# A fused attention and mixture-of-experts kernel: the four parts of a chunk's scatters moved from consecutive attention units to every second one

## The chip, the cores and the metric

The kernel runs on one core of one Trainium2 chip, as one program without collectives. The metric is the device time of one launch in microseconds (us), median over runs. One run is also profiled, and every row below comes from that profiled execution.

## What is computed

Eight sequences of 2496 tokens go through an attention with squared-ReLU scores, whose result is multiplied by `u`. All 19968 rows that come out are then sorted to one of 8 experts each. Every expert is a two-layer network, and its output is scaled by two gates and put back at the token's row.

```python
scores = (1.0 / S) * np.matmul(z, z.transpose(0, 2, 1))      # S = 2496, z: 8 x 2496 x 64
attn = np.maximum(scores, 0.0) ** 2
x = (u * np.matmul(attn, v)).reshape(B * S, D)               # D = 256
logits = x @ w_gate                                          # 8 experts
e_idx = np.argmax(logits, axis=1)
gate_w = softmax(logits)[e_idx]
eom = 1.0 / (1.0 + np.exp(-(x @ w_output_gate)))
for e in range(8):
    mask = e_idx == e
    h = np.maximum(x[mask] @ w1[e], 0.0)                     # 1024 hidden columns
    out[mask] = gate_w[mask, None] * eom[mask, e, None] * (h @ w2[e])
```

## The kernel before

**Attention stage.** A batch is cut into 5 chunks of queries (448 queries in chunk 0, 512 in the others), and a chunk is worked through in 10 units, one for every 256 keys. That makes 8 x 5 x 10 = 400 units. In a unit TensorE computes scores (L270, L271), or takes mirrored ones that were stored earlier (`take`, L355 and L385), and multiplies earlier scores with `v` (`weigh`, L403). ScalarE (ACT) applies ReLU (L272) and the square (L275) and rounds to the high half (L277, L385). VectorE (DVE) computes the low half (L281, L389). Scores are made two units ahead of the unit that weighs them.

**The tail of a chunk.** When a chunk's 10 units are done, an object of class `Tail` takes its output through a list of small steps, while the units of the next chunk run. The loop over the units calls `advance` of every live tail once per unit, just after that unit's `weigh`. Steps 0 to 9 run in the next chunk: multiply with `u` (`gate`), split, turn the rows (`rows`, L470, into the tile `xr`, of which there are two buffers), gate logits, choice of the expert (`pick`, L490 on ACT among others), `factor` (L531 and L535 on ACT), `place` (a small matmul, L556) and `scatter`, which works out each token's row number (L574). Step 10 is empty.

**The scatters.** Steps 11 to 14 are the four parts, so they fall into units 1, 2, 3 and 4 of the chunk after that. A part casts a quarter of the row numbers to integers on ACT (L581, tile `idx`, 8 buffers) and then issues four indirect DMAs on GpSimd (POOL, L585; three in two of the parts of a chunk 0). Each writes 128 rows of `xr` to `xs`, the array in memory from which the experts later load their tokens.

**What sets the order.** Every engine gets its instructions in the order in which the Python code writes them. SP issues the ordinary DMAs. GpSimd issues nothing but these scatters during attention, apart from a few preparations at the start. A step list `later` spreads the last two tails over the beginning of the expert stage.

**Expert stage.** Slots of up to 512 tokens load rows of `xs` (`load_x`, L921 and L929), and run the two layers. The first two slots' rows are already loaded inside the last two chunks of attention (units 4 of chunks 3 and 4 of the last batch). A scatter that comes behind such a load in the program waits for the load to land, as both touch `xs`.

Of the kernel before, what the change touches and what calls it, by code (L numbers as in the profile page):

```python
# [59 lines left out]

REST = S - (NCH - 1) * CH - 2 * P

TAIL = 15

N_HELD = 2

# [10 lines left out]
def attention_moe(ctx, tc, zt, zq_in, ut, v, wg, w12, out):  # L77
# [336 lines left out]
    class Tail:  # L414
# [183 lines left out]
        def advance(self):  # L598
            k = self.step
            self.step += 1  # L600
            (
                self.gate,
                lambda: (self.split(0), self.split(1)),
                self.rows,
                self.logits,
                self.turn,
                self.choose,
                self.pick,
                self.factor,
                lambda: (self.finish(), self.place()),  # L610
                self.scatter,
                lambda: None,
                lambda: self.scatter_part(0),
                lambda: self.scatter_part(1),
                lambda: self.scatter_part(2),
                lambda: self.scatter_part(3),
                lambda: None,
            )[min(k, TAIL)]()


    def t1(name, shape, dt=F32, tag=None):
        return pool.tile([1] + shape, dt, name=name, tag=tag or name)
# [247 lines left out]
    def pads():  # L870

        pad = pool.tile([P, ROW], F32, name="pad", tag="lt")
        nc.gpsimd.memset(pad, 0.0)
        nc.gpsimd.memset(pad.bitcast(I32)[:, SEG - 1 : SEG], NOTOK)
        ends = t1("ends", [E], I32)
        nc.vector.tensor_copy(out=ends, in_=carry[0][0:1])
        yield
        for e in range(E + 1):
            if e < E:
                at = nc.sync.value_load(ends[0:1, e : e + 1], min_val=e * CAP, max_val=e * CAP + N)  # L880
                seg = xs_rows[bass.ds(at, TW), :]
            else:
                seg = xs_rows[E * CAP : E * CAP + TW, :]
            it = nc.sync.dma_start(
                out=seg.rearrange("(p q) d -> p q d", q=4), in_=pad.unsqueeze(1).to_broadcast([P, 4, ROW])
            )
            tc.add_to_no_dep_group(last_scatters, it.ins)
            yield
# [291 lines left out]
    def prepare(k):  # L1180
        while to_load and to_load[0][0] - to_load[0][1] <= k:
            to_load.pop(0)[2].load()
        while to_split and to_split[0][0] <= k:
            to_split.pop(0)[2].split()

    attn = {}
    tail = nxt = o = None
    tails = []
# [23 lines left out]
    for k, (b, c, jp) in enumerate(units):  # L1212
# [33 lines left out]
        if pos == NPAIR - 1:  # L1246
            tail = nxt
            tails = [it for it in tails if it.step < TAIL] + [tail]
        prepare(k)
# [1 line left out]

    idle = lambda: None
    later = [idle] * (4 * 12)
    for k in (0, 2, 6, 10, 14):
        later[k] = tails[0].advance
    for k in (*range(1, 22, 2), 22, 29, 32, 35):
        later[k] = tail.advance
    more, fill = other_tables(), pads()
    for _ in range(29):
        later += [idle, lambda: next(more, None)]  # L1260
# [73 lines left out]
    with tc.If(used > N_MAIN + 1):  # L1334
        part = slots[last + 1 :]
# [63 lines left out]
```

## Time and profile before

| What | Value |
|---|---|
| Median of 3 runs | 2200.44 us (2196.61 to 2205.82) |
| The profiled execution's own time | 2191.03 us |
| Its span, first to last instruction | 2189.2 us |
| Mean granted TensorE clock | 0.999 of full speed |
| TensorE matmuls busy | 2163.7 us, 99% of the span |
| DVE busy | 1752.4 us, 80% |
| ACT busy | 1452.0 us, 66% |
| GpSimd busy | 940.2 us, 43% |

Busy times say how long an engine had an instruction in work, and idle time of an engine counts only where a busier one waits for it. The views used below are the page's totals, busy times by stretch of time, the list of who waited for whom, the durations and waits of one line of the kernel, and the timeline, which shows instructions in order with the idle time before them in brackets and what ended it.

### The profile page before, as it was taken

The numbers are of one execution on the slowest core, as the hardware profiler recorded it, in microseconds if no ns is written. First come the engines' busy times: TensorE is split into PE (matmuls) and PEld (weight loads), VectorE is DVE, ScalarE is ACT, GpSimd is POOL, SyncE is SP. The second block draws the span as 40 slices with busy tenths as digits, with TensorE's granted clock in tenths as the row PEclk, the third lists the DMA queues.
The fourth block names the chain that finished last, engine by engine and source line by source line (L and its number), as shares of the span: only waits on it lengthen the run. The fifth ranks groups of instructions, "written<-read, shape, count | busy, mean of one in ns | idle before, by whom it ended". The sixth has DMA issues, their size and how long they took to land. (4 is left out here: it accounts for less than half of the span.)

```text
span 2189.2 us, 35155 instructions
## 1 busy us (share of the span) xinstructions
PE 2163.7 (99%) x10207; PEld 1828.4 (84%) x10207; DVE 1752.4 (80%) x2884; ACT 1452.0 (66%) x2494; POOL 940.2 (43%) x829
## 2 busy tenths in 40 slices
PE   9999999999999999999999999999999999999998
PEld 7888788788788788888788888888888898888998
DVE  8898898898898898898898897676666766666676
ACT  8768768768778767767768765555555555555565
POOL 1365565565565564665565574321212111121222
PEclk9999999999999999999999999999999999999999
DMA  6695795794785785784784694535566766666542
GB/s 211 210 240 169 215 242 167 215 241 167 222 235 171 222 232 166 223 234 166 217 239 163 216 266 114 150 95 154 178 188 188 217 210 200 198 187 201 184 148 79
DMA packets 467738, 423.88 MB, mean 194 GB/s; under 512 B 156077, under 2 KB 366638, under 8 KB 467536
## 3 DMA queue, kind: packets, MB, share of 16 engines
q1 hardware_dynamic: 439952, 379.97, 59.3%
q0 software_dynamic: 27584, 41.58, 5.5%
q8 instruction: 82, 1.34, 0.3%
q14 instruction: 120, 0.98, 0.1%
HBM read 292.21 MB, written 158.66 MB: 206 GB/s over the span
## 5 line engine op out<-in xcount | busy, mean ns | idle before, releaser
L585 POOL DMA_INDIRECT xs<-xr,idx x624 | 766.1, 1228 | 597.8 <-ACT idx L581 422.1
L403 PE MATMUL o<-ah,v 128*128 128x512 f32 (+1 forms) x3200 | 845.8, 387 | 9.0 <-ACT ah L277 6.9
L403 PEld LDWEIGHTS o<-ah,v 128*128 128x128 f32 x3200 | 596.1, 188 | 120.7 <-ACT ah L277 10.7
L403 PE MATMUL o<-al,v 128*128 128x512 f32 (+1 forms) x1520 | 463.8, 386 | 0.5
L1012 ACT ACTIVATE hh<-sc 128x512 fp32r<-128x512 f32 (+7 forms) x328 | 190.1, 580 | 391.1 <-PE sc L1003 348.8
L1125 POOL DMA_INDIRECT out<-y,meta x156 | 159.0, 1019 | 629.1 <-ACT y L1115 558.3
L1013 DVE SCALAR_TENSOR_TENSOR hl<-sc,hh 128x512 fp32r<-128x512 f32 (+7 forms) x328 | 218.2, 665 | 262.3 <-ACT hh L1012 248.5
L1003 PE MATMUL sc<-xh,w 128*128 128x512 f32 (+8 forms) x1440 | 399.0, 362 | 1.8 <-issue 1.8
L1058 PE MATMUL o<-hh,w 128*128 128x512 f32 (+7 forms) x1184 | 400.2, 379 | 0.0
L403 PEld LDWEIGHTS o<-al,v 128*128 128x128 f32 x1520 | 283.9, 188 | 58.6 <-DVE al L281 6.6
L281 DVE TENSOR_TENSOR al<-a,ah 128x1024 fp32r<-128x1024 f32 (+1 forms) x199 | 233.1, 1171 | 111.0 <-ACT ah L277 91.0
L1003 PEld LDWEIGHTS sc<-xh,w 128*128 128x128 f32 x1440 | 258.2, 188 | 40.6 <-issue 1.3
L272 ACT ACTIVATE a<-sc 128x512 f32<-128x512 f32 (+1 forms) x398 | 207.6, 572 | 105.9 <-PE sc L271 44.1
L1058 PEld LDWEIGHTS o<-hh,w 128*128 128x128 f32 x1184 | 221.2, 188 | 38.9
L957 DVE TENSOR_TENSOR w<-raw,w 128x512 fp32r<-128x512 f32 x368 | 246.1, 680 | 2.8 <-ACT w L956 2.2
L1058 PE MATMUL o<-hl,w 128*128 128x512 f32 (+7 forms) x592 | 224.5, 379 | 0.0
L956 ACT CAST w<-raw 128x512 fp32r<-128x512 f32 x368 | 220.1, 615 | 0.0
L385 ACT CAST ah<-z 128x1024 fp32r<-128x1024 f32 x192 | 199.5, 1047 | 20.9 <-DMA z<-td 17.3
L275 ACT ACTIVATE a<-a 128x1024 f32<-128x1024 f32 (+1 forms) x199 | 203.6, 1023 | 6.3
L1003 PE MATMUL sc<-xl,w 128*128 128x512 f32 (+8 forms) x720 | 202.3, 362 | 0.0
L389 DVE TENSOR_TENSOR al<-z,ah 128x1024 fp32r<-128x1024 f32 x160 | 194.5, 1216 | 8.3 <-ACT ah L385 3.8
L270 PE MATMUL sc<-z,hl 128*128 128x512 f32 (+1 forms) x398 | 152.8, 384 | 5.0 <-ACT a L272 4.2
(201 smaller groups left out, 2395.5 us busy)
## 6 DMA issues: line engine op xcount, KB each, us to landing
raw<-in_w SPq DMA_DIRECT2D x368, 256.0 KB
z<-td SPq DMA_DIRECT2D x647, 128.0 KB
td<-t SPq DMA_DIRECT2D x160, 512.0 KB
raw<-in_v SPq DMA_DIRECT2D x80, 256.0 KB
u<-in_ut SPq DMA_DIRECT2D x32, 512.0 KB
ym<-yd SPq DMA_DIRECT2D x126, 128.0 KB
sx<-xs SPq DMA_DIRECT2D x120, 128.0 KB
yd<-yt SPq DMA_DIRECT2D x30, 512.0 KB
```

The costliest lines, as they stand in the source:

```text
L272: nc.scalar.activation(out=a[:, q, :w], in_=sc[:, :w], func=AF.Relu)
L275: nc.scalar.activation(out=a[:, :, :w], in_=a[:, :, :w], func=AF.Square)
L281: nc.vector.tensor_tensor(out=al[:, :, :w], in0=a[:, :, :w], in1=ah[:, :, :w].bitcast(F32), op=ALU.subtract)
L385: nc.scalar.copy(out=ah, in_=z)
L389: nc.vector.tensor_tensor(out=al, in0=z, in1=ah.bitcast(F32), op=ALU.subtract)
L403: nc.tensor.matmul(out=o[d][:, :w], lhsT=vv[:, q, d * P : (d + 1) * P], rhs=rhs, start=begins and q == 0 and k == 0, stop=ends and q == 1 ...
L585: it = nc.gpsimd.indirect_dma_start(out=xs[:, :], out_offset=bass.IndirectOffsetOnAxis(ap=idx[:, n - first : n - first + 1], axis=0), in_= ...
L956: nc.scalar.copy(out=ww[:, 0], in_=wr)
L957: nc.vector.tensor_tensor(out=ww[:, 1], in0=wr, in1=ww[:, 0].bitcast(F32), op=ALU.subtract)
L1003: nc.tensor.matmul(out=hp[:, at : at + n], lhsT=wb[2 * d + f // 4][:, ww, fs], rhs=xx[:, d, :], start=k == 0, stop=k == 5,)
L1013: nc.vector.scalar_tensor_tensor(out=lo, in0=hp[:, 0:used], scalar=0.0, in1=ho.bitcast(F32), op0=ALU.max, op1=ALU.subtract)
L1058: nc.tensor.matmul(out=y, lhsT=st, rhs=mv, start=f == 0 and k == 0, stop=f == 7 and k == 2)
```

## The change

The list of steps in `advance` gets three more empty steps, one before each of the parts 1, 2 and 3. In the attention stage the parts then stand at steps 11, 13, 15 and 17, that is at units 1, 3, 5 and 7 of the chunk. The last two tails, which run in the expert stage, get their parts by direct calls at the same places of `later` at which they stood before.

```diff
-TAIL = 15
+TAIL = 18
...
                 self.scatter,
                 lambda: None,
                 lambda: self.scatter_part(0),
+                lambda: None,
                 lambda: self.scatter_part(1),
+                lambda: None,
                 lambda: self.scatter_part(2),
+                lambda: None,
                 lambda: self.scatter_part(3),
                 lambda: None,
             )[min(k, TAIL)]()
...
     later = [idle] * (4 * 12)
-    for k in (0, 2, 6, 10, 14):
-        later[k] = tails[0].advance
-    for k in (*range(1, 22, 2), 22, 29, 32, 35):
+    for k in range(1, 22, 2):
         later[k] = tail.advance
+    for part in range(4):
+        later[2 + 4 * part] = lambda part=part: tails[0].scatter_part(part)
+        later[(22, 29, 32, 35)[part]] = lambda part=part: tail.scatter_part(part)
```

On ACT the casts `idx<-row` of the parts 1, 2 and 3 come later. This is chunk 0 of batch 4, from unit 4 to unit 7. `a`, `z` and `ah` are scores, `dl` and `hot` belong to the tail of the chunk before. Before:

```order
L581 ACTIVATE idx<-row 128x4
L272 ACTIVATE a<-sc 128x448 x2
L275 ACTIVATE a<-a 128x2x448
L197 CAST z<-raw 128x512
L367 ACTIVATE z<-sc 128x192 x2
L369 ACTIVATE z<-z 128x2x192
L387 CAST ah<-z 128x2x448
L490 ACTIVATE ex<-dl 128x128
L272 ACTIVATE a<-sc 128x448 x2
L275 ACTIVATE a<-a 128x2x448
L277 CAST ah<-a 128x2x448
L531 COPY both<-hot_103 64x136
```

And the same stretch after the change:

```order
L275 ACTIVATE a<-a 128x2x448
L581 ACTIVATE idx<-row 128x4
L197 CAST z<-raw 128x512
L367 ACTIVATE z<-sc 128x192 x2
L369 ACTIVATE z<-z 128x2x192
L387 CAST ah<-z 128x2x448
L490 ACTIVATE ex<-dl 128x128
L272 ACTIVATE a<-sc 128x448 x2
L275 ACTIVATE a<-a 128x2x448
L277 CAST ah<-a 128x2x448
L581 ACTIVATE idx<-row 128x4
L531 COPY both<-hot_103 64x136
```

The cast that closed unit 4 (part 3) now stands in unit 7, directly ahead of the copy L531, and part 2 stands in unit 5. The order on TensorE, VectorE, SP and GpSimd is the same in both kernels.

On GpSimd one thing differs all the same, in the last batch, where a scatter comes behind the first load of an expert's rows. The piece shows the scatters of chunk 3 of that batch with the semaphores that each waits for (`DMAHW`: loads that SP issued, `DMASW`: earlier scatters, `Activation`: the cast):

```order
 L585 DMA xs<-xr,idx 657408x66 [waits DMASW6_49]
 L585 DMA xs<-xr,idx 657408x66 [waits DMASW7_49]
-L585 DMA xs<-xr,idx 657408x66 [waits DMASW0_49,Activation_49]
-L585 DMA xs<-xr,idx 657408x66 [waits DMASW1_49]
-L585 DMA xs<-xr,idx 657408x66 [waits DMASW2_49]
-L585 DMA xs<-xr,idx 657408x66 [waits DMASW3_49]
-L585 DMA xs<-xr,idx 657408x66 [waits DMASW4_49,Activation_49]
-L585 DMA xs<-xr,idx 657408x66 [waits DMASW5_49]
-L585 DMA xs<-xr,idx 657408x66 [waits DMASW6_49]
-L585 DMA xs<-xr,idx 657408x66 [waits DMASW7_49]
 L585 DMA xs<-xr,idx 657408x66 [waits DMAHW2_49,DMAHW1_49,DMAHW6_49,DMAHW0_49,DMAHW7_49,DMASW0_49,Activation_49]
```

The wait for the load moves from the first scatter of the next chunk's tail eight rows up, to the first scatter of part 2 of this one, since parts 2 and 3 now come behind the load.

## Rows read from the trace of the kernel before

**Rows 1.** The page's first part: busy time, share of the span, instructions.

```profile
PE 2163.7 (99%) x10207; PEld 1828.4 (84%) x10207; DVE 1752.4 (80%) x2884; ACT 1452.0 (66%) x2494; POOL 940.2 (43%) x829
```

**Rows 2.** Busy times, attention stage: us, PE, PEld, DVE, ACT, POOL, clock, DMA.

```profile
30.00:1318.00 1288.00, 1275.49 (x5787) 1064.05 (x5786) 1137.43 (x1867) 951.95 (x1546) 732.00 (x592) 1.00 0.72 210
```

**Rows 3.** Who waited for whom, TensorE, 30 to 1318 us (us, times, longest).

```profile
PE o L403 <- ACT ah L277: 6.9, 9, 1.6
PE sc L270 <- ACT a L272: 3.5, 2, 3.3
PE mp L556 <- ACT both L531: 0.8, 1, 0.8
```

**Rows 4.** Timeline of two TensorE holes (start, duration, engine, line, instruction).

```profile
728.20 1.09 ACT L272 ACTIVATE a<-sc 128x512 f32<-128x512 f32 x2 [2.68 <-PE mp L556]
...
731.51 0.74 PE L403 MATMUL o<-ah,v 128*128 128x512 f32 x2 [0.95 <-ACT ah L277]
...
855.49 0.50 PE L270 MATMUL sc<-z,hl 128*128 128x512 f32 x1 [3.30 <-ACT a L272]
```

**Rows 5.** Timeline of GpSimd: one tail's 16 scatters (first, last), and five others.

```profile
702.81 0.97 POOL L585 DMA_INDIRECT xs<-xr,idx  x1 [12.04 <-ACT idx L581]
...
725.66 1.67 POOL L585 DMA_INDIRECT xs<-xr,idx  x1 [0.30 <-issue]
736.89 1.19 POOL L585 DMA_INDIRECT xs<-xr,idx  x1 [9.57 <-ACT idx L581]
...
1262.65 0.97 POOL L585 DMA_INDIRECT xs<-xr,idx  x1 [9.82 <-ACT idx L581]
...
1280.79 1.06 POOL L585 DMA_INDIRECT xs<-xr,idx  x1 [0.31 <-DMA meta<-xs]
...
1291.14 1.01 POOL L585 DMA_INDIRECT xs<-xr,idx  x1 [3.30 <-ACT idx L581]
...
1315.32 0.97 POOL L585 DMA_INDIRECT xs<-xr,idx  x1 [0.30 <-issue]
```

**Rows 6.** Line L585 on GpSimd: durations (ns min/median/max), and its idle time before.

```profile
L585 POOL DMA_INDIRECT xs<-xr,idx x624: 966/1067/2367, 83.1 to 1385.7; - x156
...
  ACT idx L581: 422.1, 54
  issue: 164.1, 532
```

**Rows 7.** Line L581 on ACT: durations, and who waited for it.

```profile
L581 ACT ACTIVATE idx<-row x160: 185/198/211, 82.6 to 1377.9; 128x4 int32<-128x4 f32 x144, 128x3 int32<-128x3 f32 x16
...
  POOL xs L585: 422.1, 54
```

**Rows 8.** Timeline of ACT in chunk 0 of batch 4.

```profile
676.59 1.07 ACT L272 ACTIVATE a<-sc 128x448 f32<-128x448 f32 x2 [0.93 <-issue]
...
682.87 0.56 ACT L367 ACTIVATE z<-sc 128x192 f32<-128x192 f32 x2 [0.57 <-PE o L403]
...
686.65 0.31 ACT L490 ACTIVATE ex<-dl 128x128 f32<-128x128 f32 x1 [1.69 <-DVE mx L482]
...
689.69 0.30 ACT L531 COPY both<-hot 64x136 bf16<-64x136 bf16 x1
690.77 0.22 ACT L535 ACTIVATE eo<-osel 128x16 f32<-128x16 f32 x1 [0.78 <-issue]
```

**Rows 9.** Timeline of DVE: writes of `xr` two tails behind, for two tails.

```profile
745.71 1.21 DVE L470 STREAM_TRANSPOSE xr<-u 128x1024 f32<-128x1024 f32 x1
...
1326.09 1.23 DVE L470 STREAM_TRANSPOSE xr<-u 128x1024 f32<-128x1024 f32 x1
```

**Rows 10.** Timeline of SP in the last batch: the first expert slot's loads.

```profile
1274.06 2.58 SPq L921 DMA_DIRECT2D sx<-xs  x4
1276.84 0.48 SPq L929 DMA_DIRECT2D meta<-xs  x1
```

**Rows 11.** Line L389 on DVE: durations (ns min/median/max).

```profile
L389 DVE TENSOR_TENSOR al<-z,ah x160: 1178/1218/1273, 43.2 to 1311.4; 128x1024 fp32r<-128x1024 f32 x160
```

## The prediction, as it was made before the result

> **What bounds the kernel now.** I began with the page's totals [rows 1]: TensorE has a matmul in work for 2163.7 of 2189.2 us. So the time is TensorE's, and a change that leaves its instructions alone can only close or open holes between them. Next I split the span by stage [rows 2], since the change touches the attention stage alone. From 30 to 1318 us TensorE is busy 1275.5 of 1288.0 us. The holes there are 12.5 us in all, and no rearrangement of other engines can give back more than that. ACT is busy 952 us of this stretch, 74%, and DVE 1137 us, 88%, so both have slack on average.
>
> Then I asked what TensorE waited for in this stretch [rows 3]. The named waits are few: 6.9 us for the high half of the scores from ACT (9 times), 3.5 us for a score bank that ACT had not yet emptied (2 times), 0.8 us for ACT's copy L531. Neither the scatters nor the casts for them appear. The timeline shows what two of these holes look like [rows 4]. At 731.51 TensorE waits 0.95 us for ACT, and ACT itself had stood idle for 2.68 us before it began that chain at 728.20, waiting for TensorE. At 855.49 the hole is 3.30 us, behind one late ACTIVATE. I read them as rings between TensorE and ACT about score buffers, near chunk ends, and what fell late was not ACT's quarter-microsecond work.
>
> Last I looked at the moved work itself. A tail's 16 scatters run back to back on GpSimd [rows 5]: the first starts at 702.81 us, the last ends at 725.66 + 1.67 = 727.33, so 24.5 us for 16, or 1.53 us for one. The next tail's first one starts at 736.89, so a chunk lasts 34.1 us and a unit 3.4 us. Over all, a scatter takes 1.07 us in the median, and most gaps are issue gaps: 164.1 us over 532 of them, 0.31 us each [rows 6]. The casts take 0.198 us, and only GpSimd waits for them [rows 7].
>
> **The change part by part.**
>
> *Scatters on GpSimd.* Before, a part falls due every 3.4 us but takes 4 x 1.53 = 6.1 us. So GpSimd falls behind at once, and its queue already spreads the four parts evenly over 24.5 us, some seven units. With the change a part falls due every 6.8 us. Part 3 is due six units, 20.4 us, after part 0, and ends 6.1 us later: 26.5 us after the start, against 24.5. The scatters hardly move. They get short pauses of 0.7 us between the parts and end about 2 us later. The forecast rests on this: **the spacing that the change writes into the program is about the one that GpSimd's own speed gives now.** What covers the 2 us is the distance to the next write of the same `xr` buffer: 745.71 - 727.33 = 18.4 us for this tail, and the shortest that I found is 1326.09 - (1315.32 + 0.97) = 9.8 us, in the last batch [rows 5, 9]. Without that cover DVE would wait in `rows`, and behind it in DVE's queue the low halves of scores. Cost: 0.
>
> *Casts on ACT.* Of 160 casts, 40 are first parts and 6 more belong to the last two tails, which keep theirs; the other 114 move. Their sum is 114 x 0.198 = 22.6 us of ACT time, taken from units 2 to 4 and put into units 3 to 7. No ACT work is added. In chunk 0 of batch 4, the kind in which ACT is closest to late, the new places of parts 2 and 3 are followed by idle time of ACT: 0.57 us before L367, 1.69 before L490, 0.78 before L535 [rows 8]. A cast of 0.2 us put in front of these shortens the idle time and delays nothing behind it. One of the old places, after the cast of unit 3, was followed by 0.93 us. What could be late next is L531, as in chunks 0 part 3 now stands directly before it, and TensorE's L556 needs it. TensorE waited for L531 once, 0.8 us [rows 3]. If the cast delayed it in all of the chunks 0 of batches 1 to 7, that would be 7 x 0.2 = 1.4 us. From below, taking two casts away in front of the scores of units 4 and 5 could shorten the waits on ACT by as much. I take 0.3 us of loss, as one wait for L531 exists and one such cast lies before it. The ends are wide: nothing gained below 12.5 us (all holes of the stage) and nothing lost above 22.6 us (every moved cast on the path).
>
> *The wait for loads in the last batch.* The first slot's loads are issued at 1274.06 to 1277.3 us [rows 10], and the scatter that waits for the last of them now starts at 1280.79 [rows 5]. With the change the same wait falls on part 2's first scatter. That part comes due four units after part 0 of this tail, which started at 1262.65; the next tail's starts ten units later, at 1291.14, so a unit is 2.85 us here and part 2 is due at about 1274.1. GpSimd could stand until 1280.8, 6.7 us. Behind it in its queue are only scatters. The idle time before the next tail, 3.30 us, takes up half of that, and the next tail inherits some 3 us. The 9.8 us above still cover 2 + 3 us. The second slot's load in the next chunk is met in the same way, a few units later. Cost: 0, bound 5 us if that cover failed.
>
> *The two last tails.* The calls stand at the same steps of `later`. Step 0, whose advance is left out, called an empty step. Cost: 0.
>
> *DVE beside GpSimd.* A scatter takes from 966 to 2367 ns [rows 6], so something stretches it, while the long two-input subtractions of DVE stay between 1178 and 1273 ns in all 160 of one line [rows 11]. So DVE is not held up here, and a different overlap would change the scatters' length alone, which nobody waits for. I put it at 0, and bound it by 160 x (1273 - 1178) ns = 15 us if each of these met its worst. The Trainium skill (SBUF — State Buffer, section "Who interferes with whom") says that VectorE instructions with two inputs in SBUF and GpSimd instructions that read SBUF exclude each other on a shared port, and that the one that starts second is blocked until the first is done. By that rule a scatter that starts first would hold a subtraction for up to a whole scatter, and the moved scatters could cost DVE time in new places. The trace bears out half of it: scatters are stretched up to 2.4 times, the subtractions by 8% at most.
>
> **The sum.** 0 + 0.3 + 0 + 0 + 0 = 0.3 us on the profiled execution's own 2191.03 us. That execution stands 9.4 us below the median of the three runs, 2200.44. Added to the median, and rounded, the forecast is **2200 us**. A measurement of this kernel can tell about 0.5%, or 11.0 us, from no change.
>
> **The rivals.**
>
> *The spreading relieves ACT or the DMA queues, and TensorE's holes close (faster).* For it: ACT loses casts in front of the scores of units 3 to 5, and the holes of rows 3 all end on ACT. Against it: the holes stand at chunk ends, and the two in rows 4 follow idle time of ACT of 2.68 us and more. If half the holes closed, the time is 2194; if all did, 2200.4 - 12.5 = 2188. Only nearly all of them would pass 0.5%.
>
> *A cast lands in front of urgent ACT work (slower).* Place: units 5 and 7, ahead of scores that TensorE takes within two units. Price: 0.198 us for each moved cast that lies on the path. It decides from 11.0 / 0.198 = 56 of 114 on, one in every second place; the time with all on the path is 2223. Against it: the idle time of ACT behind both new places in rows 8, and 26% idle in the stage.
>
> *GpSimd's tail end runs into the next write of `xr` (slower).* Place: `rows` on DVE. It decides when the scatters end over 9.8 us later than now in the tightest chunk and over 18 in a usual one; I worked out 2, and up to 5 at the end of the stage. If they did by 0.5 us more in each of 38 chunks, the time is 2219.
>
> *DVE is held by scatters in new places (slower).* By the 15 us above the time would be 2215. It needs the subtractions at their maximum everywhere, and then TensorE behind them.
>
> *The change does less than it says.* As the queue spreads the scatters already, this is my forecast's own mechanism, with the same time.
>
> **How the numbers follow.** The forecast has 0.84, all within 0.5% but for some 0.02 on either side for runs that differ by themselves. Holes closing has 0.08, half of it beyond 0.5%. The cast rival has 0.05, GpSimd's end 0.02 and DVE 0.01, and half of these three go beyond 0.5%. That makes faster 0.02 + 0.04 = 0.06, slower 0.02 + 0.04 = 0.06, same 0.88. The range takes in most of the holes closed (10 of 12.5 us) below and 44% of the moved casts on the path (10 of 22.6 us) above, and with them the spread of the runs, whose lowest is 2196.6 and whose profiled one is 2191.0: 2190 to 2210.
>
> **What would show it.** In the profile after, a tail's 16 scatters should last about 26 us, with GpSimd waiting for casts about 0.5 to 1 us before parts 1 to 3; the attention stage's TensorE busy time should stay at 1275 us, with holes of 11 to 15 us. The last batch should show one wait of GpSimd of some us for `sx` or `meta`. The prediction is wrong if TensorE's waits for ACT in this stage grow or shrink by more than 5 us, if `rows` waits for a scatter, or if the scatters' total moves TensorE in any way.

## The result, and the profile after

The changed kernel took 2177.61 us (median of 4 runs, 2174.70 to 2182.29), the kernel before 2201.99 beside it (4 runs, 2196.61 to 2205.82). The ratio is 0.9908, with a 95% interval of 0.9887 to 0.9929: faster by 0.92%, where no change was forecast. The profiled execution took 2175.11 us (span 2173.3), against 2191.03. So the two traces account for 15.9 us, while the medians differ by 24.4: the profiled execution of the kernel before was quicker than its other runs.

Later sets of runs, on chips 15, 13 and 6, did not repeat this size: 0.9989 (0.9977 to 1.0002) beside a kernel before of 2176.45 us, and twice 1.0000 (0.9991 to 1.0009) beside one of 2166.2. So there are two questions: what the change cured, and why it was there to cure only in some sets.

The page's totals and the stretch of [rows 1, 2] after the change. The second row has the columns of rows 2, with the DMA's GB/s last.

```profile
PE 2156.4 (99%) x10207; PEld 1829.1 (84%) x10207; DVE 1754.9 (81%) x2884; ACT 1451.3 (67%) x2494; POOL 930.4 (43%) x829
```

```profile
30.00:1318.00 1288.00, 1283.76 (x5856) 1078.16 (x5856) 1154.40 (x1888) 961.00 (x1565) 728.81 (x599) 1.00 0.73 212
```

TensorE's idle time in the stretch fell from 12.5 to 4.2 us, and 69 more matmuls fit into it (5856, before 5787). TensorE's busy time fell as well, by 7.3 us, with the same 10207 matmuls. From the first `weigh` to that of unit 399 it took 1305.5 us before and 1287.8 after, 17.7 less, while all that follows, to the last matmul, grew by 2.3. Who waited for whom, TensorE, same stretch, after [rows 3]:

```profile
PE o L403 <- ACT ah L277: 1.9, 1, 1.9
PE sc L1006 <- DVE hl L1016: 1.6, 1, 1.6
```

The nine waits for the high half are one. To see why, look at what ACT waited for. A row of the same view for ACT, the kernel before:

```profile
ACT a L272 <- PE mp L556: 16.5, 9, 2.7
```

In these places L272 (ReLU of a score bank) has one semaphore to wait for, TensorE's, and what it needs of TensorE is L271, the last matmul into its bank. That it is put down to L556 nine times means that L271 was long over: 728.20 in [rows 4] is such a case. Its L271 had started at 723.23 and its row ended at 723.62, TensorE had gone through over 4 us of other matmuls, and ACT had been free since 725.52. After the change the same place in batch 2 (402.21 before, idle 2.66 us) reads like this, on ACT and on GpSimd:

```profile
394.23 0.21 ACT L535 ACTIVATE eo<-osel 128x16 f32<-128x16 f32 x1 [0.92 <-DVE osel L526]
394.35 1.07 ACT L272 ACTIVATE a<-sc 128x512 f32<-128x512 f32 x2
```

```profile
371.76 0.97 POOL L585 DMA_INDIRECT xs<-xr,idx  x1 [7.19 <-ACT idx L581]
...
379.66 1.83 POOL L585 DMA_INDIRECT xs<-xr,idx  x1 [1.43 <-ACT idx L581]
...
386.07 1.55 POOL L585 DMA_INDIRECT xs<-xr,idx  x1 [0.30 <-issue]
...
392.35 0.97 POOL L585 DMA_INDIRECT xs<-xr,idx  x1 [0.71 <-ACT idx L581]
...
396.56 0.97 POOL L585 DMA_INDIRECT xs<-xr,idx  x1 [0.30 <-issue]
```

ACT goes on at once. The train of scatters is hardly longer (25.8 us), but GpSimd now stands 1.43 and 0.71 us before two of the parts.

I call a **late wait** one in which ACT stood idle for over 0.3 us ahead of L272, L367 or L378 and then started over 0.3 us after the row of the last matmul into its bank had ended. Its length is the part of ACT's idle time that lies behind that row's end. A **train** is the scatters of one tail. The kernel before has 23 late waits, 35.9 us in all; after the change there are 2, 4.8 us. In 22 of the 23 the trace has a record of TensorE's semaphore within 0.03 us of ACT's start, so ACT started on this signal and on no other engine's. Of the 23, 11 (24.4 us) ended 0.8 to 1.4 us after the last scatter of a train, the others while one of its scatters ran.

### The profile page after: what moved, and what is told of

It reads as the page before. It is cut to its first block, busy times and chain, and to the rows that moved or that the text cites. A ratio compares the mean times of both kernels' runs of the same rounds, so it can differ in the third digit from the quotient of the medians.

```text
span 2173.3 us, 35149 instructions
## 1 busy us (share of the span) xinstructions
PE 2156.4 (99%) x10207; PEld 1829.1 (84%) x10207; DVE 1754.9 (81%) x2884; ACT 1451.3 (67%) x2494; POOL 930.4 (43%) x829
## 5 line engine op out<-in xcount | busy, mean ns | idle before, releaser
L585 POOL DMA_INDIRECT xs<-xr,idx x624 | 756.1, 1212 | 592.2 <-ACT idx L581 387.6
L272 ACT ACTIVATE a<-sc 128x512 f32<-128x512 f32 (+1 forms) x398 | 207.7, 573 | 97.5 <-PE sc L271 48.2
L389 DVE TENSOR_TENSOR al<-z,ah 128x1024 fp32r<-128x1024 f32 x160 | 194.8, 1218 | 9.1 <-issue 4.8
L277 ACT CAST ah<-a 128x1024 fp32r<-128x1024 f32 (+1 forms) x150 | 151.9, 1013 | 4.8
```

What stands on the lines that cost most here:

```text
L272: nc.scalar.activation(out=a[:, q, :w], in_=sc[:, :w], func=AF.Relu)
L389: nc.vector.tensor_tensor(out=al, in0=z, in1=ah.bitcast(F32), op=ALU.subtract)
L585: it = nc.gpsimd.indirect_dma_start(out=xs[:, :], out_offset=bass.IndirectOffsetOnAxis(ap=idx[:, n - first : n - first + 1], axis=0), in_= ...
```

## The experiments

The theories, by the letters that the expectations use. A: the pauses on GpSimd between the parts close TensorE's holes. B: the casts in front of scores at units 2 to 4 make ACT late. C: it matters what the end of a train meets. X and Y: the kernel before has one time, or several levels. D is A made sharper after the first two sets: while a train of scatters runs, TensorE's signals reach ACT late, on some chips, and a pause lets them through. E: a later train collides with other work on any chip.

The kernels of a set ran on one chip, beside the same runs of the kernel before. The first set's chip has no number on record. The late waits are those of the one execution of each kernel that was profiled; the times are medians of 4 to 27 runs.

| Set, chip | Kernel | us | Ratio to before (95%) | Late waits, us |
|---|---|---|---|---|
| first | before / after | 2202.0 / 2177.6 | 0.9908 (0.9887 to 0.9929) | 23, 35.9 / 2, 4.8 |
| 0 | before, no profile | 2175.6 | | |
| 0 | one cast | 2181.0 | 1.0030 (1.0014 to 1.0045) | 15, 17.9 |
| 0 | change + spare casts | 2172.3 | 0.9983 (0.9970 to 0.9996) | 3, 4.1 |
| 0 | units 4, 5, 6, 7 | 2248.4 | 1.0317 (1.0290 to 1.0344) | 33, 79.2 |
| 0 | units 1, 4, 7, 9 | 2173.7 | 0.9988 (0.9977 to 0.9999) | 7, 8.2 |
| 13 | before / after | 2166.2 / 2166.7 | 1.0000 (0.9991 to 1.0009) | 0 / 0 |
| 15 | before / after | 2176.5 / 2172.8 | 0.9989 (0.9977 to 1.0002) | 10, 12.6 / 0 |
| 15 | eight parts | 2170.9 | 0.9977 (0.9965 to 0.9990) | 0 |
| 15 | before + pauses | 2168.1 | 0.9964 (0.9950 to 0.9978) | 0 |
| 12 | before, no profile | 2175.3 | | |
| 12 | units 4, 5, 6, 7 | 2252.7 | 1.0368 (1.0346 to 1.0390) | 29, 72.2 |
| 12 | the same + pauses | 2202.5 | 1.0132 (1.0114 to 1.0150) | 1, 0.4 |
| 12 | before + one pause | 2177.7 | 1.0014 (1.0005 to 1.0023) | 7, 9.6 |
| 12 | before + short pauses | 2170.7 | 0.9978 (0.9969 to 0.9987) | 0 |
| 6 | before + pauses | 2165.8 | 0.9999 (0.9990 to 1.0008) | 0 |
| 6 | after | 2165.9 | 1.0000 (0.9991 to 1.0009) | 0 |
| 6 | change + pauses | 2166.7 | 1.0001 (0.9992 to 1.0010) | 0 |

**One cast for four (of the kernel before).**

```diff
-            idx = pool.tile([P, 4], I32, name="idx", bufs=8)
-            nc.scalar.activation(
-                out=idx[:, 0 : end - first], in_=self.row[:, first:end], func=AF.Copy, scale=4.0
-            )
+            if part == 0:
+                self.idx = pool.tile([P, NB], I32, name="idx", bufs=3)
+                nc.scalar.activation(
+                    out=self.idx[:, 0 : self.w // 32], in_=self.row[:, 0 : self.w // 32], func=AF.Copy, scale=4.0
+                )
```

> The kernel before, but a tail's row numbers are cast by one ACTIVATE at unit 1 in place of four at units 1 to 4. The scatters stay at their places and, as GpSimd works through them back to back, keep their times. Theory A (TensorE's holes close because the scatters get pauses between the parts): no pauses here, so about 2200 us, ratio 0.997 to 1.003, and the waits of L272 for a matmul that ended over 0.3 us earlier stay near the 23 of before. Theory B (the casts in front of scores at units 2 to 4 make ACT late): three of four casts are gone, so about 2178, ratio 0.988 to 0.993, and nearly all of these waits are gone.

Three of four casts are gone from ACT, and nothing is gained: 1.0030, if anything slower, with 15 late waits. Theory B falls. One of the late waits, on ACT, chunk 1 of batch 3, at the same unit as above:

```profile
560.58 0.60 ACT L272 ACTIVATE a<-sc 128x512 f32<-128x512 f32 x1 [1.74 <-PE mp L556]
```

**Spare casts at units 2 and 4 (of the changed kernel).** `spare` casts four columns into a tile that nothing reads.

```diff
                 lambda: self.scatter_part(0),
-                lambda: None,
+                self.spare,
                 lambda: self.scatter_part(1),
-                lambda: None,
+                self.spare,
```

> The changed kernel (parts at units 1, 3, 5, 7) with a spare cast of the same size, which nothing reads, at units 2 and 4: ACT then has a cast at every place of before, and two more. Theory A (pauses between the scatters): the pauses are kept, so about 2178 us, ratio 0.988 to 0.993. Theory B (casts at units 2 to 4 make ACT late): they are back, so 2195 or more, ratio 0.997 to 1.003, with waits of L272 for long-ended matmuls back at some 20.

Only 3 late waits, with casts at every old place and two more, and a time slightly below that of the kernel before. The ratio is not A's 0.988 to 0.993; the kernel before itself ran 26 us faster than beside the change, and that was the first hint that it has more than one level.

**Parts at units 4, 5, 6, 7.** Against the list of the kernel before, with `later` as in the change:

```diff
                 lambda: None,
+                lambda: None,
+                lambda: None,
+                lambda: None,
                 lambda: self.scatter_part(0),
```

> Parts at units 4, 5, 6 and 7: one unit apart as before, but three units later, so that a tail's scatters run back to back over units 4 to 11. Theory A (pauses between the parts): none, so about 2200 us, ratio 0.996 to 1.004. Theory B (casts in front of the scores of units 3 to 5): those at units 2 and 3 are gone, two late ones stay, so 2178 to 2190, ratio 0.988 to 0.995. A third reading, C (what counts is which fetches of stored scores the end of the train meets): the train ends in the next chunk, so the holes move from units 9 to units 1 and 2 of the chunk after, total 2185 to 2205.

No theory expected this: 3.2% slower. The late waits rose to 33. One of the longest, in batch 2, on ACT, and behind it on TensorE:

```profile
381.13 1.09 ACT L272 ACTIVATE a<-sc 128x512 f32<-128x512 f32 x2 [6.63 <-remote]
```

```profile
381.78 0.80 PE L270 MATMUL sc<-z,hl 128*128 128x512 f32 x1 [4.35 <-ACT a L272]
```

The train's last scatter ended at 379.53, 1.6 us earlier. The stage took 1350.6 us. Some 15.4 us of that are TensorE's clock: behind six holes of this kind the granted clock stood at 0.50 for 3.4 or 6.8 us.

**Parts at units 1, 4, 7, 9 (against the changed kernel).**

```diff
                 lambda: self.scatter_part(0),
                 lambda: None,
+                lambda: None,
                 lambda: self.scatter_part(1),
                 lambda: None,
+                lambda: None,
                 lambda: self.scatter_part(2),
```

> Parts at units 1, 4, 7 and 9: pauses between the parts of some 4 us, 4 us and 0.7 us in place of 0.7 us. Theory A (pauses): at least the gain of the change, 2170 to 2180 us, ratio 0.986 to 0.992. Theory B (casts off units 2 to 4): one of them stays at unit 4, so 2178 to 2185, ratio 0.988 to 0.994. Theory C (place of the train's end): the train ends at units 10 to 11, so the holes stand elsewhere, 2180 to 2205.

The longer pauses bring no more than shorter ones: 0.9988 and 7 late waits, now all at units 1 and 3, where the longer train has its end. That speaks for C's place as well as for A. All seven stand in a stretch of eight scatters that run back to back, or up to 1.0 us behind it.

**The two kernels again, on another chip.**

> The kernel before, unchanged, profiled again, because its runs beside the first four experiments took 2175.6 us (27 runs) where the four beside the change took 2202.0. Theory X (its time is one number, and one of the two sets was disturbed): the profile shows the 23 waits of L272 and L367 for long-ended matmuls, 36 us in all, as the first one did. Theory Y (the kernel before has two levels, and these waits come or go with where and how the program was loaded): a profile at 2175 us shows fewer than 12 of them, and the attention stage lasts 1285 to 1292 us in place of 1305.5; one at 2200 shows some 20 of them.

> The changed kernel, unchanged, beside more runs of the kernel before. Theory X (the gain belongs to the change): ratio 0.988 to 0.994 again. Theory Y (most of the gain is the level that the kernel before fell on beside it): ratio 0.996 to 1.001, 2170 to 2178 us.

Y holds in kind, though at a level that it had not named (it expected 2170 to 2178 us): the kernel before takes 2166.2 us here, without one late wait, and the change does nothing. Its totals, and ACT at the place shown above:

```profile
PE 2152.8 (99%) x10207; PEld 1828.9 (85%) x10207; DVE 1755.4 (81%) x2884; ACT 1452.0 (67%) x2494; POOL 939.5 (43%) x829
```

```profile
394.10 0.22 ACT L535 ACTIVATE eo<-osel 128x16 f32<-128x16 f32 x1 [0.91 <-DVE osel L526]
394.23 1.07 ACT L272 ACTIVATE a<-sc 128x512 f32<-128x512 f32 x2
```

Busy times from 30 to 1290 us, this run and then the first kernel before (columns as in rows 2):

```profile
30.00:1290.00 1260.00, 1260.00 (x5763) 1061.07 (x5761) 1137.36 (x1858) 950.26 (x1545) 727.60 (x589) 1.00 0.74 213
```

```profile
30.00:1290.00 1260.00, 1247.49 (x5661) 1041.01 (x5660) 1113.88 (x1827) 938.39 (x1522) 711.42 (x576) 1.00 0.71 210
```

The scatters are the same on both chips (765.7 us busy there, 766.1 in the first profile), and so is the granted clock (0.999). From the first `weigh` to that of unit 399 this run took 1282.8 us. All six profiles of the two kernels and of the one with three pauses that show no late wait lie at 1282.7 to 1283.3, so this is what the stage takes with nothing late. The first kernel before lost 22.7 us against it, and the changed one 5.0. Three kernels below have no late wait and still take longer: change + pauses 1284.3 and short pauses 1285.6, both with waits for `xr`, and eight parts 1287.5. The last lost its 4.7 us in one place of the last batch (1275 to 1281 us), where TensorE, ACT and DVE all stood idle for reasons that the trace doesn't show.

**The two kernels a third time, eight parts, and pauses on GpSimd alone.** Eight parts, `scatter_part(0)` to `scatter_part(7)`, stand at units 1 to 8:

```diff
-            first, end = part * self.w // 128, (part + 1) * self.w // 128
-            idx = pool.tile([P, 4], I32, name="idx", bufs=8)
+            first, end = part * self.w // 256, (part + 1) * self.w // 256
+            idx = pool.tile([P, 2], I32, name="idx", bufs=16)
```

The pauses go into the kernel before, with all casts and parts at their old places:

```diff
+            if part:
+                gap = pool.tile([P, 64], F32, name="gap", bufs=1)
+                for _ in range(6):
+                    nc.gpsimd.memset(gap, 0.0)
             for n in range(first, end):
```

> The kernel before, a third time. Theory D (while a train of scatters runs on GpSimd, TensorE's signals reach ACT and DVE late on some chips and at once on others, and the time goes by that): at 2170 us or more the profile shows waits of L272 for matmuls that ended over 0.3 us earlier, 8 to 25 of them, each ended 0.7 to 1.6 us after a train's last scatter; at 2167 or less it shows none. Theory X (the time has one level, other runs were disturbed): 2200 us with 23 of these waits, or 2166 with none, and no relation of the waits to the scatters.

> The changed kernel, a third time. Theory D: ratio 0.988 to 0.998 if the kernel before shows such late waits beside it (the pauses between the parts let the signals through), and 0.999 to 1.001 if it shows none. Theory B (the casts' places on ACT): ratio 0.99 in either case.

> Eight parts of two scatters at units 1 to 8 (one cast each): a train of 16 becomes eight of 2 with some 0.3 us of pause in each. Theory D: at most as many late waits as the changed kernel, 0 to 4, and a time within 0.3% of it, below that of the kernel before where that has late waits. Theory B (casts in front of scores make ACT late): casts at every unit from 1 to 8, so no gain, ratio 0.998 or more to the kernel before.

> The kernel before with its casts and parts where they were; ahead of the scatters of parts 1, 2 and 3 GpSimd alone does six memsets of a spare tile, about 1.1 to 1.5 us in which no scatter is issued. Theory D: the pauses let the signals through as in the changed kernel, so the late waits of the kernel before fall to under a quarter and the time comes within 0.3% of the changed kernel's; on a chip without late waits 0.999 to 1.002. Theory B: the casts are at their old places, so the time of the kernel before, 0.998 to 1.002, with its late waits.

The kernel before has 10 late waits on this chip (12.6 us). Not each ended behind a train, as I had written: 6 of 10 did, 0.6 to 1.3 us behind, and the others while a scatter ran. The profiles of the change, of eight parts and of the pauses show 0, and the pauses alone bring most: 0.9964, at 2168.1 us. GpSimd and ACT in this kernel, chunk 1 of batch 2:

```profile
385.00 0.97 POOL L589 DMA_INDIRECT xs<-xr,idx  x1 [0.30 <-issue]
385.96 1.22 POOL L587 MEMSET gap<- 128x64 f32 x6
387.84 0.97 POOL L589 DMA_INDIRECT xs<-xr,idx  x1 [0.66 <-ACT a L272]
```

```profile
394.44 0.21 ACT L535 ACTIVATE eo<-osel 128x16 f32<-128x16 f32 x1 [0.91 <-DVE osel L526]
394.56 1.07 ACT L272 ACTIVATE a<-sc 128x512 f32<-128x512 f32 x2
```

Between scatters 1.87 us pass (385.97 to 387.84), and GpSimd is at work in most of it. So GpSimd need not rest, and ACT's program is that of the kernel before. D holds on this point.

For the change itself D's 0.988 to 0.998 is missed: its interval reaches 1.0002, so on this chip a gain is not shown. Nor does its one profile show that it is free of late waits, for that execution was the fastest of its 11 (2168.07 of up to 2179.47 us), while the paused kernel's five lie between 2168.1 and 2168.7. Another count of the same traces says more. Where TensorE's signals are held up, several come at once (the last section has an example), so I count those that the trace records within 60 ns of the one before, from 30 to 1295 us. There are 25 in the kernel before, 17 in the changed one, 17 with eight parts, and none with the pauses. GpSimd's catching up leaves the changed kernel some scatters back to back: with under 0.5 us between them there are still 9 stretches of 16, 8 of 12 and 8 of 8, and 14 of the 17 signals came 0.9 to 1.1 us behind a stretch of 12. In the paused kernel all stretches but two are of four or fewer. So the change only thins the held-up signals; with stretches of four there are none.

**How much pause, and the late train again.** The late train gets three memsets ahead of parts 1, 2 and 3. The other two put theirs into the kernel before: one pause of six memsets under `if part == 2`, and short ones inside the loop over a part's scatters:

```diff
             for n in range(first, end):
+                if n % 2 == 0 and n:
+                    gap = pool.tile([P, 64], F32, name="gap", bufs=1)
+                    for _ in range(3):
+                        nc.gpsimd.memset(gap, 0.0)
```

> Parts at units 4, 5, 6 and 7 again, as in the run that was 3.2% slower with 29 late waits (79 us). Theory D (signals of TensorE come late while a train of scatters runs, on some chips): on a chip that shows late waits in any of these four, 1.02 to 1.04 again; on one that shows none, 0.998 to 1.005, since nothing else in the kernel is late. Theory E (the later train collides with the next write of the tile of rows, or with other work of the next chunk, whatever the chip): 1.02 to 1.04 on every chip.

> Parts at units 4, 5, 6 and 7, and GpSimd does three memsets of a spare tile, about 1.2 us without a scatter, ahead of parts 1, 2 and 3. The train gets some 3 us longer and ends still later. Theory D: the late waits fall from 29 (79 us) to under 10 (20 us), and the time from 1.03 to under 1.01 of the kernel before. Theory E: a longer train collides more, 1.03 or above.

> The kernel before with one pause of six memsets in the middle of a tail, ahead of part 2, in place of the three that brought 0.9964. Theory D, if the backlog is let out at any pause of 1.9 us: a train of 8 is short enough, so late waits at 0 to 5 and 0.996 to 0.999 beside a kernel before that has them. If each stretch of 8 already builds a backlog: half of the late waits stay, 0.998 to 1.000.

> The kernel before with three memsets ahead of every second scatter, about 1.2 us between scatters at seven places of a tail in place of 1.9 us at three. Theory D: no late waits, 2166 to 2170 us on any chip, at or below 0.9964 of the kernel before where that has late waits. If a pause has to be longer than 1.2 us to let signals through: late waits stay, 0.998 to 1.000.

(The 29 late waits that the first expectation gives the earlier run are 33 in the table.) Pauses in the late train take 29 late waits to 1 and 50 us off its time, so most of its loss was the same thing. 1.0132 is left, above D's bound of 1.01. That is E's collision, but the pauses brought it: only the train that they make longer runs into the next write of `xr`. DVE's line of that write, late train with pauses, then without; the last two columns are its idle time before and what ended it:

```profile
L470 DVE STREAM_TRANSPOSE xr<-u 128x1024 f32<-128x1024 f32 (+1 forms) x40 | 47.8, 1195 | 46.5 <-DMA xs<-xr,idx 29.2 <-issue 17.3
```

```profile
L470 DVE STREAM_TRANSPOSE xr<-u 128x1024 f32<-128x1024 f32 (+1 forms) x40 | 47.6, 1191 | 0.0
```

In each of the eight batches TensorE then stands at unit 5 of chunk 4, 2.0 to 5.4 us (from matmul to matmul, over the usual distance), 27.0 us in sum, behind the `al` that stands behind this write. In batch 1 DVE waits like this, and TensorE 3.08 us, until 325.07:

```profile
322.67 1.25 DVE L470 STREAM_TRANSPOSE xr<-u 128x1024 f32<-128x1024 f32 x1 [5.73 <-issue]
```

The stage takes 1317.9 us, 35.1 above the 1282.8 with nothing late. Behind four of the eight holes the granted clock then stands at 0.50 for 3.4 us, which I estimate at 4 x 1.7 = 6.8 us. The two together make 33.8 of the 35.1.

One pause is not enough: against the profiles of the kernel before on other chips (it has none on this one), the late waits in the chunks 1 are gone, those at the end of the chunks 0 stay (5 of the 7), and the time is no better (1.0014, where D had at most 1.000). So a stretch of eight scatters behind a pause still makes them, and 26 signals within 60 ns. Seven pauses of 1.2 us end them, but their train is longer, DVE waits 14.4 us for it at `xr`, and the time is 2170.7 us (0.9978, just outside D's 2170 and 0.9964), where three pauses of 1.87 us had 2168.1 on the other chip.

**The cure on a chip that doesn't need it.** The paused kernel and the changed one again, and the changed one with three memsets ahead of parts 1, 2 and 3.

> The kernel before with six memsets on GpSimd ahead of parts 1, 2 and 3, again. Theory D: 2166 to 2169 us whatever the kernel before takes beside it, with no late waits, and a spread of runs under 3 us.

> The changed kernel, a fourth time. Theory D: its pauses are shorter (0.3 to 0.7 us), so 0 to 5 late waits stay where the kernel before has them: 2168 to 2176 us, between the paused kernel and the kernel before; 0.9995 to 1.0005 where there are none.

> The changed kernel with three memsets on GpSimd ahead of parts 1, 2 and 3. Theory D: no late waits, 2166 to 2169 us like the kernel with pauses alone, so nothing is left that the places of the parts could bring beside the pauses.

This chip shows no late wait in any of the three, and they are equal to the kernel before. No cost of the pauses can be measured here (0.9999). The kernel before with three pauses is the best version found: it beats the kernel before on chip 15, is below the changed kernel there (2168.1 and 2172.8 us, their intervals only just touching), and is level with both on chip 6.

## Why the prediction was wrong

The changed kernel's 2177.6 us lies below the range of 2190 to 2210. The step that put it there is the price of the scatters, 0, which rests on a wrong reading of the holes.

*Reading of the holes.* This step failed first. I took the holes of [rows 3, 4] for rings between TensorE and ACT near chunk ends. They were late waits. The sign was in rows that I quoted: ACT idle for 2.68 us "<-PE mp L556" ahead of an L272 that needs only L271, which had ended over 4 us before. By the prediction's own sign, TensorE's waits for ACT fell by more than 5 us: from 11.2 us in [rows 3] to 1.9.

*"The spacing that the change writes is about the one that GpSimd's own speed gives now. Cost: 0."* The spacing was right: 25.8 us for the tail shown, forecast 26.5, with pauses of 0.7 and 1.4 us. The price was wrong. I priced the scatters by who waits for them, and left out that signals between other engines come late while they run. Where the sum has 0, the stage became 17.7 us shorter, with 2 late waits in place of 23. The pauses, which I wrote off as short, are what acts: memsets that make pauses of 1.87 us with nothing else moved end the late waits, and fewer casts do not.

*"No rearrangement can give back more than 12.5 us."* Failed. The change gave back 17.7 us of the stage, and it had 22.7 us to give. TensorE's busy time of the same 10207 matmuls is 2163.7 us in [rows 1] and 2152.8 on the chip without late waits: 10.9 us of loss lay inside "busy". Two rows show how. The matmul behind the hole at 855.49 in [rows 4] takes 0.50 us, where the median of its line is 0.39. And behind that hole the granted clock stands at 0.50, the 1.2 GHz level, for 3.4 us: TensorE gets through 15 matmuls in 4.60 us, and through 25 in the next 5.00.

```profile
855.40:860.00 4.60, 4.51 (x15) 3.78 (x16) 2.13 (x3) 4.50 (x9) 0.00 (x0) 0.63 0.00 0
860.00:865.00 5.00, 5.00 (x25) 4.38 (x24) 3.96 (x11) 4.31 (x6) 0.00 (x0) 1.00 0.45 164
```

The weight loads show the loss better. In 30 to 1290 us they are busy 1061.1 us there and 1041.0 in the first profile, 1.9% less, which I estimate at 23.8 of 1260 us. The Trainium skill (Perfetto Trace Analysis, section "Identifying the Most-Contended Engine") says that TensorE's busy share of matmuls is no good measure of how close a kernel is to the roofline, because they are pipelined, and names the busy share of weight loads as one of two better ones. These rows agree: matmul idle time showed 12.5 us of a loss of 22.7, weight loads 23.8.

*Casts on ACT, 0.3 us.* Right in kind: with casts at every old place and two more there are 3 late waits, and with three of four gone there are 15, on one chip. No price above 0 was shown for them.

*Wait for the loads in the last batch, the two last tails, `xr`.* No cost was seen in the changed kernel: DVE's line L470 has no idle time in it. GpSimd did stand in the last batch, 5.46 us ahead of the scatter at 1263.16, where up to 6.7 was forecast. What `xr` costs when the train does reach it stands above, 27 us; the rival was sound, and a train of 26 us from unit 1 on does not reach it.

*DVE beside GpSimd.* Not tried by itself. DVE's L389 took 1218 ns in the mean on the chip without late waits, 1216 in the first profile. What stretches the scatters is not shown.

*The rivals.* The one that came was "relieves ACT or the DMA queues, and TensorE's holes close". ACT was not the means, and that the DMA queues were is not shown either way. I gave it 0.08, and half of that for over 0.5%. Half the holes closing would have been 2194 and all 2188; it was 2177.6.

*The base.* 2200 us was the level of the kernel before in one set. On the five chips of the later sets it took 2166.2 to 2176.5. Where nothing is late, the forecast's ratio of 1.000 is what was measured, twice; the holes that it misread are not there.

**What stays open.** Why the first set gained 0.92% and the next with late waits 0.1%: the first kernel before had 23 of them and the third 10, but which chip the first was is not on record. Why the signals are late, and what differs between the chips; as each known chip was met in one set alone, the chip and the set cannot be told apart either. Whether it is the making of the scatters' transfers or their data that holds signals up was not tried, nor whether the recording of the trace takes a part: on the chips with late waits it holds some 30% fewer signals of the same program. Nor is it shown that the memsets do no more than keep the scatters apart: no run without them has stretches of four throughout. Nor is it shown that the signal is late rather than the result itself, as the ends of matmuls in the rows are modelled.

## What to carry to other kernels

Where an engine's wait is put down to an instruction that it does not depend on, look up the one that it does: if that one's row ended long before, the two engines alone do not explain it, and what else ran then is the suspect. A back-to-back train of indirect DMAs can be such a suspect although nobody waits for it; try short pauses in it, as long as its end stays clear of the next write of its source. And run the unchanged kernel on more than one chip before a difference below 1% is believed: here the kernel before alone differed by 1.7% between sets, and by 0.5% between chips 13 and 15. One profile is one execution: compare its time with the other runs before its count of waits is taken for the kernel's.

## What the runs showed of the hardware

Whether TensorE's signals can come late went with the set, and so with its chip, whatever the kernel. In the trace's own records of semaphores, the kernel before has 1133 signals of TensorE from 30 to 1295 us on chip 13, none within 60 ns of the one before. The first profile has 799, although about as many instructions give one (1119, and 1136 on chip 13), and 56 of them come within 60 ns of the one before: none stands between 717.24 and 728.11, and then six in 0.27 us, 0.8 us after the last scatter had ended at 727.33. No kernel changes this number by much: it is 772 to 808 on chip 15, with or without late waits, 772 to 836 on all chips that showed late waits, and 1124 to 1136 on chips 13 and 6. The loss isn't only in attention: what follows unit 399's first `weigh`, to the last matmul, took 867.1 to 867.4 us on chips 13 and 6, and 868.7 us or more in every other profile.

GpSimd can be given 720 memsets, 115.8 us of busy time, without any cost in time that could be measured on chip 6 (0.9999).

Behind long holes of TensorE the granted clock fell to half (0.50) for 3.4 or 6.8 us: once in the attention stage of the first kernel before, six times in each profile of the late train, and four times in the late train with pauses. In the other profiles it stayed at full speed through that stage.
